# Attention and GELU layer on one core: the first matrix's sums right behind its casts, loads in the weights' buffers, temporaries in unread weights

## The chip, the core and the metric

The kernel runs on one core of a Trainium2 chip. Its engines work side by side, each on its own instruction stream: PE (TensorE, matmuls), DVE (VectorE), ACT (ScalarE), POOL (GpSimd) and SP (SyncE, which here only issues DMAs). They meet at semaphores. PE writes to PSUM, of which the kernel uses eight buffers in turn; the other engines move results from there to SBUF. The metric is the device time of one execution in microseconds.

## The reference

Two layers one behind the other. First a linear attention with decay, in 4 batches, 8 heads, 768 positions, 64 channels, blocks of 64 positions:

```python
for b in range(nb):
    intra = einsum(qb, kb) * Dmask              # scores inside the block, masked with powers of lam
    intra = einsum(intra, vb)
    inter = einsum(qb * lam_pow, kv_state)      # what earlier blocks left
    out[block] = intra + inter
    kv_state = lam_block * kv_state + einsum(kb * rev_pow, vb)
```

Then a dense layer pair on its output x (3072 tokens of 512 features), with a hidden width of 2048:

```python
h = x @ w_in                                    # 512 x 2048
g = 0.5 * h * (1.0 + tanh(c * (h + 0.044715 * h * h * h)))
return g @ w_out                                # 2048 x 512, float32
```

## The kernel before

**Steps.** The attention goes through 24 steps. A step is half of the heads (four) over 256 positions, two chunks of 128. `load_step` brings q, k and v of a step in float32 (256 KB each, 2 KB in each partition), by three DMAs from SP. `cast_q` (DVE, L282) and `cast_k` (ACT, L295) make float16 of q and k, `scale_v` (POOL, L266) of v. q and k are transposed by PE (`stage_t`, L321, for steps up to 7) or by a transposing DMA (L303, from step 8). `scores` (L350) gives S = k q; `causal` (DVE, L360) multiplies by the mask and writes the float16 tile PT. `products` (L385 to L408) or, for two steps at once, `burst` (L436 to L461) multiplies v by PT and adds the state's part. `update` makes the next state t (DVE, L503 and L506) and its float16 form u (POOL, L513). `x_out` (ACT, L487) writes x transposed.

**Groups.** The dense layers go in seven groups of steps. Both matrices are cast to float16 once (`cast_win`, L110 and L108; `cast_wout`, L118 and L120). Group 0 multiplies plainly. From group 1 the second product is done with seven block products in place of eight (`product`, L640), for which sums of blocks of w_out are made (`sum_wout`, L133), and sums of the GELU's output (`sum_g`, L610). In groups 5 and 6 the first product goes the same way (`seven`, L739): it needs four sums of blocks of w_in, each made in two parts on DVE (`sum_win`, L151, eight instructions on 128x1024), sums of blocks of x (`sum_x`, L718), and temporaries that carry partial results between the seven products (`copied`, L751 and L753; `added`, L761). Which blocks it reads is in a table, by (columns half, rows half) or by the number of a sum:

```python
I_SUMS = {1: ((1, 0), ALU.add, (1, 1)), 2: (1, ALU.subtract, (0, 0)),
          3: ((0, 0), ALU.subtract, (1, 0)), 4: ((0, 1), ALU.subtract, 2)}
X_FACTORS = {1: ((0, 0), (0, 0)), 2: ((0, 1), (1, 0)), 3: (4, (1, 1)), 4: ((1, 1), 4),
             5: (1, 1), 6: (2, 2), 7: (3, 3)}
```

**Order.** Nothing is planned automatically: every instruction is pinned to the program order of its engine, and the order is written out by hand at the end of the kernel. The dense layers' pieces lie in a list, `filler`; `fill(n)` emits the next n of them between the parts of the attention, so that PE has work while other engines prepare a step. Dependencies between engines are found by the framework from the regions that the instructions touch.

**Buffers.** A pool hands out tiles by tag; a new tile takes the buffer of an old one of the same tag when all accesses to that one are done. Before, q, k and v have four buffers each (tags q32, k32, v32 of pool `ld`, 24 KB in each partition). The float32 weights arrive in `wst`, four tags of 8 KB: w_in's column quarters in w0 to w3, then w_out's row quarters 0, 2, 1, 3 in w0, w1, w2, w3. Later w0 and w1 hold the sums of the GELU, w2 and w3 the sums of w_in (`ws`). The temporaries of `seven` rotate through q32 and k32. Loads up to step 8 stand at the head of SP's order, behind the weights.

Of the kernel before, what the change touches and what calls it, by code (L numbers as in the profile page):

```python
# [8 lines left out]
FP32 = mybir.dt.float32  # L9
FP16 = mybir.dt.float16  # L10
AF = mybir.ActivationFunctionType
ALU = mybir.AluOpType
# [3 lines left out]
def kernel(  # L16
# [10 lines left out]
    nc = tc.nc  # L27
    pin = tc.keep_in_program_order
    P = 128
    B, H, S, D = q.shape  # L30
    SB = 256
    NSB = S // SB
    HH = H // 2
    DM = H * D
    DFF = moe_w_in.shape[1]
# [6 lines left out]
    const = ctx.enter_context(tc.tile_pool(name="const", bufs=1))  # L42
    w16p = ctx.enter_context(tc.tile_pool(name="w16", bufs=1))
    wst = ctx.enter_context(tc.tile_pool(name="wst", bufs=1))
    ld = ctx.enter_context(tc.tile_pool(name="ld", bufs=4))
    a16p = ctx.enter_context(tc.tile_pool(name="a16", bufs=5))
    qkp = ctx.enter_context(tc.tile_pool(name="qkp", bufs=5))
    ptp = ctx.enter_context(tc.tile_pool(name="ptp", bufs=3))
    ucp = ctx.enter_context(tc.tile_pool(name="ucp", bufs=3))
    ubp = ctx.enter_context(tc.tile_pool(name="ubp", bufs=4))  # L50
    xtp = ctx.enter_context(tc.tile_pool(name="xtp", bufs=3))
    gtp = ctx.enter_context(tc.tile_pool(name="gtp", bufs=2))
    mtp = ctx.enter_context(tc.tile_pool(name="mtp", bufs=1))
# [4 lines left out]
    ld32 = {}  # L58

    def load_step(s, names="qkv"):  # L60
        b, r = divmod(s, 2 * NSB)
        sb, half = divmod(r, 2)
        ts = ld32.setdefault(s, [])
        for nm, src in (("q", q), ("k", k), ("v", v)):
            if nm not in names:
                continue
            t = ld.tile([P, HH, 2, D], FP32, tag=nm + "32", name=f"{nm}32_{s}")
            rows = src[b, half * HH : (half + 1) * HH, sb * SB : (sb + 1) * SB, :]
            queue = nc.scalar if (nm, s) == ("v", 0) else nc.sync
            pin(queue.dma_start(out=t[:].rearrange("p h j d -> p h (j d)"),  # L70
                                in_=rows.rearrange("h (p j) d -> p h (j d)", j=2)))
            ts.append(t)

    w_in16 = w16p.tile([P, NC, DFF], FP16)
    w_out16 = w16p.tile([P, NF, DM], FP16)
# [2 lines left out]
    HF, HE = NF // 2, DM // 2  # L78
# [65 lines left out]
    def sum_win(m, j, eng):  # L144

        if not wi_sum:
            wi_sum.extend(wst.tile([P, 2, 2, DFF // 2], FP16, tag=f"w{2 + i}", name=f"ws{i}")
                          for i in range(2))
        a, op, b = I_SUMS[m]
        cs, fs = slice(0, 2), slice(512 * j, 512 * j + 512)  # L150
        pin(eng.tensor_tensor(w_in_block(m, cs, fs), w_in_block(a, cs, fs),  # L151
                              w_in_block(b, cs, fs), op))
# [96 lines left out]
    def wide(t):  # L249
        return t.rearrange("p j h d -> p h j d")  # L250

    def decay(t, s):
        hs = halves[s % 2]
        return t[:, hs, :].unsqueeze(3).to_broadcast([P, HH, 2, D])
# [8 lines left out]

    def scale_v(s):
        tv = a16p.tile([P, 2, HH, D], FP16, tag="v16", name=f"v16_{s}")
        pin(nc.gpsimd.tensor_tensor(wide(tv[:]), ld32[s][2][:], decay(dv, s), ALU.mult))  # L266
        a16[s] = a16[s] + (tv,)

    def prep_qk(s):
# [5 lines left out]
        cast_k(s)  # L275

    def cast_q(s):
        q32 = ld32[s][0]
        tqk = a16p.tile([P, 2, 2, HH, D], FP16, tag="qk16", name=f"qk16_{s}")
        tq, tk = tqk[:, 0], tqk[:, 1]  # L280
        q_eng = nc.gpsimd if s == 3 else nc.vector
        pin(q_eng.tensor_tensor(wide(tq), q32[:], decay(dq, s), ALU.mult))  # L282
        if s == 0:
            inverse(halves[0])
            odd(halves[1])
            inverse(halves[1])
        a16[s] = (tq, tk)
        whole_qk[s] = tqk

    def cast_k(s):  # L290
        tk, k32 = a16[s][1], ld32[s][1]
        if s == 4:
            pin(nc.vector.tensor_copy(out=wide(tk), in_=k32[:]))
        else:
            pin(nc.scalar.activation(out=wide(tk), in_=k32[:], func=AF.Copy))  # L295

    whole_qk = {}

# [245 lines left out]
    def queue_group(g, lead=0, per_set=0):  # L544
# [177 lines left out]
        def release():  # L722
            while pending:
                pending.pop(0)()

        def seven(m, k):

            st = of_set.setdefault(k, {})
            for name in {1: "X" if k == 0 else "XW", 2: "W", 5: "Y"}.get(m, ""):
                key = name + str(k % 2) if name == "X" else name  # L730
                if key not in hbank:
                    hbank[key] = ps_M.tile([P, 2, SB], FP32, tag="M", name="H" + name)
                st[name] = hbank[key]
            dst = st[{2: "W", 5: "Y", 3: "Y"}.get(m, "X")]
            a, b = X_FACTORS[m]
            for i in range(2):
                f = 2 * k + i
                for c in range(2):
                    pin(nc.tensor.matmul(  # L739
                        dst[:, i, :],  # L740
                        w_in_block(a, slice(c, c + 1), slice(f * P, f * P + P))[:, 0],
                        x_block(b, slice(c, c + 1))[:, 0],
                        start=((m in (1, 5) or (m, k) == (2, 0)) and c == 0 and i == 0),
                        stop=(m in (2, 3, 4) and c == 1),
                        skip_group_check=True))

            def copied(name, tag, eng):
                t = ld.tile([P, HH, 2, D], FP32, tag=tag, name=f"{name}_{g}_{k}")
                t = t[:].rearrange("p h j d -> p (h j d)").rearrange("p (i t) -> p i t", i=2)
                if eng is nc.scalar:  # L750
                    pin(nc.scalar.activation(out=t, in_=dst[:], func=AF.Copy))  # L751
                else:
                    pin(eng.tensor_copy(out=t, in_=dst[:]))  # L753
                st[name] = t

            def gelu(F, T, src):
                pin(nc.scalar.activation(out=gT[:, 2 * k : 2 * k + 2, F, T * SB : T * SB + SB],  # L757
                                         in_=src, func=AF.Gelu_apprx_tanh))

            def added(F, T, name):  # L760
                pin(nc.vector.tensor_tensor(st[name], dst[:], st[name], ALU.add))  # L761
                pending.append(lambda src=st[name]: gelu(F, T, src))

            if m == 1 and k == 0:
                copied("m1", "q32", nc.scalar)
            elif m == 1:
                pin(nc.scalar.activation(out=st["W"][:], in_=dst[:], func=AF.Copy))
            elif m == 2 and k == 0:  # L770
                added(0, 0, "m1")
            elif m == 2:
                pending.append(lambda: gelu(0, 0, dst[:]))
            elif m == 5:
                copied("q", "q32", nc.scalar)
                release()
            elif m == 6:
                copied("u2", "k32", nc.vector)
                release()
            elif m == 3:  # L780
                added(0, 1, "u2")
            elif m == 7:
                added(1, 1, "q")
            elif m == 4:
                pending.insert(0, lambda: gelu(1, 0, dst[:]))
            if k == HF // 2 - 1 and m in (3, 7, 4):
                release()

# [193 lines left out]
    cast_win(2, 0, 256, 128)  # L982
    cast_win(2, 256, 512)
    cast_win(3)
    DVE, ACT, POOL = nc.vector, nc.scalar, nc.gpsimd
    cast_wout(0, (POOL, POOL))
    fill(8)
# [38 lines left out]
    for n, (a, b, c, d) in FILL.items():  # L1026
        stage_t(n)
        fill(a + (n == 10))
        if n == 8:
            cast_q(n + 2)  # L1030
            fill(1)
            cast_k(n + 2)
            transpose_dma(n + 2)
        else:
            prep_qk(n + 2)
        if n < 11:
            load_step(n + 4, "qkv" if n < 10 else "qk")
        if n == 9:
            store_pair(1)
        if n == 11:  # L1040
            scale_v(13)
            load_step(14, "v")
            load_step(16, "qk")
        elif n == 9:
            scale_v(11)
        elif n == 10:
            scale_v(12)
            load_step(15, "qk")
        elif n == 12:
            scale_v(14)  # L1050
        fill(b + (n == 8) - (n == 10))
        R(n, n - 1, keep=n == 8)
        fill(c)
        if n == 8:
            update(n, 0)
            scale_v(n + 2)
            fill(2)
        U(n)
        if n == 12:
            prep_qk(15)  # L1060
            load_step(15, "v")
            load_step(16, "v")
            scale_v(15)
        fill(d)
        if n > 8:
            sum_win((n - 7) // 2, (n - 1) % 2, nc.vector)

    cast_qk(16)
    load_step(17, "qk")
# [21 lines left out]
    fill(1)  # L1091
    U(17)
    fill(1)
    sum_win(3, 0, nc.vector)
    fill(2)
    prep(19)
    sum_win(3, 1, nc.vector)
    fill(2)
    sum_win(4, 0, nc.vector)
    fill(2)  # L1100
    sum_win(4, 1, nc.vector)
    fill(2)
    prep_qk(20)
    fill(1)
# [56 lines left out]
```

## Time and profile before

| | |
|---|---|
| runs of the kernel | 198.87, 198.85, 200.48 us; median 198.87 |
| the profiled execution | 198.79 us, of it 197.0 in the span |
| PE's granted clock | 1.00 |
| busy: PE, DVE, ACT, POOL | 97%, 76%, 61%, 38% of the span |
| HBM read and written | 27.26 MB and 6.29 MB |

The span is the stretch from the first to the last recorded instruction. A view of groups has one row for each line of the kernel, engine and operation; "idle before" is the time that the engine waited just ahead of it, with what ended the wait. A timeline merges like instructions that follow each other: start, duration of all, engine, line, what is written from what, the count, and in brackets the idle time before. The chain of work that ended last is followed back from the last instruction; it names for each stretch of time the work that set the end. Instructions of one engine overlap by some hundredths of a microsecond, so the distance from start to start is a little less than a duration. PEld is PE's loading of the stationary operand. SPq is the issuing of a DMA by SP.

### The profile page before, as it was taken

Reading aid. Unit: us, or ns where it says so; the run is one execution under the profiler, and the core shown is the slowest. Engines: PE = TensorE matmul, PEld = TensorE weight load, DVE = VectorE, ACT = ScalarE, POOL = GpSimd, SP = SyncE. Lnnn points to the kernel's source line nnn. Section 1 sums busy time; section 2 is a strip of 40 time slices with the busy share of each in tenths; the row PEclk is TensorE's granted clock in tenths of the full one; section 3 lists DMA queues with packets and bytes.
Section 4 is the critical chain, followed back from the end, with each engine's and each line's share of the span. In section 5 each row is a group of like instructions: output and inputs, shape, how many; then the busy total and the mean of one; then the engine's idle time right before and its main releaser. Section 6 shows DMA issues by size and latency. Waiting matters only on the chain.

```text
span 197.0 us, 5913 instructions
## 1 busy us (share of the span) xinstructions
PE 191.2 (97%) x2431; PEld 140.1 (71%) x2431; DVE 149.0 (76%) x291; ACT 121.1 (61%) x249; POOL 74.4 (38%) x85
## 2 busy tenths in 40 slices
PE   8979999999999999999999999999999999999993
PEld 2556544446888888654688764578888888888882
DVE  4797722889999889859999927999656987487620
ACT  3663878357874685686845378844867746679221
POOL 6594213457554931169754517165002030002000
PEclk9999999999999999999999999999999999999999
DMA  5999999999999999999996998400211300020205
GB/s 167 292 324 384 387 383 386 300 285 297 259 220 248 257 333 231 213 238 288 226 294 132 274 310 202 92 7 0 53 67 42 107 6 2 0 110 29 77 19 198
DMA packets 62810, 38.13 MB, mean 194 GB/s; under 512 B 18624, under 2 KB 55744, under 8 KB 62784
## 3 DMA queue, kind: packets, MB, share of 16 engines
q1 hardware_dynamic: 62240, 37.50, 74.3%
q8 instruction: 19, 0.31, 0.7%
q10 hardware_dynamic: 544, 0.26, 0.5%
q14 instruction: 7, 0.06, 0.1%
HBM read 27.26 MB, written 6.29 MB: 170 GB/s over the span
## 4 chain that ended last, share of the span: by engine, by line
PE 89%; SPq 4%; DMA 4%; ACT 0%; issue 0%
PE Hps L561 25%; PE MX L640 18%; PE MY L640 9%; PE HX L739 7%; PE O2ps L576 7%; PE MW L640 4%; DMA wi<-in_moe_w_in_dram 4%; SPq L70 4%; PE HY L739 4%; PE S L350 3%; PE Hps L838 3%; PE HW L739 2%; PE OK L408 2%; PE O L461 1%; PE O L436 1%; PE OK L399 1%
## 5 line engine op out<-in xcount | busy, mean ns | idle before, releaser
L561 PE MATMUL Hps<-xT,w_in 128*128 128x512 f16 (+1 forms) x288 | 50.5, 332 | 0.0
L513 POOL TENSOR_TENSOR u<-t,lumask 128x256 f16<-128x256 f32 x40 | 30.9, 788 | 40.7 <-DVE t L506 27.0
L561 PEld LDWEIGHTS <-w_in 128*128 128x128 f16 x288 | 27.9, 98 | 19.1
L565 ACT ACTIVATE gT<-Hps 128x512 f16<-128x512 f32 x56 | 33.5, 598 | 11.6 <-PE Hps L561 11.1
L360 DVE TENSOR_TENSOR PT<-S,mask 128x512 f16<-128x512 f32 x48 | 30.3, 680 | 7.8 <-PE S L350 7.8
L266 POOL TENSOR_TENSOR v<-v,dv 128x512 f16<-128x512 f32 x24 | 28.7, 1197 | 15.2 <-DMA v<-in_v_dram 14.0
L640 PEld LDWEIGHTS <-gs 128*128 128x128 f16 x320 | 31.2, 98 | 3.6
L640 PEld LDWEIGHTS <-gT 128*128 128x128 f16 x240 | 23.3, 98 | 3.2 <-ACT gT L565 0.2
L640 PE MATMUL MX<-w_sum,gs 128*128 128x256 f16 x160 | 21.4, 273 | 0.0
L692 POOL TENSOR_TENSOR o<-u,q 128x512 f32<-128x512 f32 (+1 forms) x5 | 6.3, 1252 | 36.7 <-ACT u L657 36.7
L282 DVE TENSOR_TENSOR qk<-q,dq 128x512 f16<-128x512 f32 x23 | 19.1, 833 | 0.8 <-DMA q<-in_q_dram 0.7
L295 ACT ACTIVATE qk<-k 128x512 f16<-128x512 f32 x23 | 14.4, 625 | 7.4 <-DMA k<-in_k_dram 7.3
L610 DVE TENSOR_TENSOR gs<-gT 128x1024 f16<-128x1024 f16 (+1 forms) x24 | 16.9, 711 | 1.6 <-ACT gT L565 1.6
L576 PE MATMUL O2ps<-w_out,gT 128*128 128x512 f16 x64 | 14.6, 379 | 0.0
L487 ACT ACTIVATE xT<-OK 128x256 f16<-128x256 f32 x26 | 9.9, 452 | 7.0 <-PE OK L408 6.5
L739 PEld LDWEIGHTS <-ws 128*128 128x128 f16 x128 | 12.5, 98 | 1.6 <-issue 0.2
L487 ACT ACTIVATE xT<-O 128x256 f16<-128x256 f32 x22 | 8.0, 461 | 5.8 <-PE O L461 4.9
L657 ACT ACTIVATE u<-MX 128x256 f32<-128x256 f32 x18 | 6.9, 384 | 7.4 <-PE MX L640 7.3
L576 PEld LDWEIGHTS <-gT 128*128 128x128 f16 x64 | 6.1, 98 | 6.6
L350 PEld LDWEIGHTS <-qkT 64*64 64x64 f16 x384 | 6.0, 106 | 6.8 <-issue 3.6
L640 PE MATMUL MY<-w_out,gs 128*128 128x256 f16 x80 | 10.7, 273 | 0.0
L753 DVE COPY u<-HX 128x512 f32<-128x512 f32 x8 | 5.5, 688 | 6.8 <-ACT gT L757 4.3
(98 smaller groups left out, 318.4 us busy)
## 6 DMA issues: line engine op xcount, KB each, us to landing
q<-in_q_dram SPq DMA_DIRECT2D x24, 256.0 KB, 4.9
k<-in_k_dram SPq DMA_DIRECT2D x24, 256.0 KB, 5.0
v<-in_v_dram SPq DMA_DIRECT2D x23, 256.0 KB, 5.2
out_dram<-o SPq DMA_DIRECT2D x23, 256.0 KB, 4.3
wo<-in_moe_w_out_dram SPq DMA_DIRECT2D x4, 1024.0 KB, 9.4
wi<-in_moe_w_in_dram SPq DMA_DIRECT2D x4, 512.0 KB, 7.1
wi<-in_moe_w_in_dram SPq DMA_DIRECT2D x2, 1024.0 KB, 12.5
v<-in_v_dram ACTq DMA_DIRECT2D x1, 256.0 KB, 4.3
```

The lines of the kernel that those rows point to most:

```text
L266: pin(nc.gpsimd.tensor_tensor(wide(tv[:]), ld32[s][2][:], decay(dv, s), ALU.mult))
L282: pin(q_eng.tensor_tensor(wide(tq), q32[:], decay(dq, s), ALU.mult))
L295: pin(nc.scalar.activation(out=wide(tk), in_=k32[:], func=AF.Copy))
L360: pin(nc.vector.tensor_tensor(t[:, hl].rearrange("p b c d -> p b (c d)"), Sps[:].rearrange("p b c d -> p b (c d)"), mask[:].unsqueeze(1).t ...
L487: pin(nc.scalar.activation(out=d, in_=o, func=AF.Copy))
L513: pin(nc.gpsimd.tensor_tensor(u[:], state[half][:].unsqueeze(2).to_broadcast([P, 2, 2, D]), lumask[:, 2 * half : 2 * half + 2, :].unsqueez ...
L561: pin(nc.tensor.matmul(by_block(Hps[:, i, :]), w_in16[:, c, f * P : (f + 1) * P], x(c), start=(c == 0), stop=(c == NC - 1)))
L565: pin(nc.scalar.activation(out=dst, in_=Hps[:], func=AF.Gelu_apprx_tanh))
L576: pin(nc.tensor.matmul(O2[tau][0][:], gT[:, f % HF, f // HF, tau * P : (tau + 1) * P], w_out16[:, f, :], start=(n == 0), stop=(n == NF - 1)))
L610: pin(nc.vector.tensor_tensor(g_rows(m, i), g_rows(a, i), g_rows(b, i), op))
L640: pin(nc.tensor.matmul(dst, lhsT, rhs, start=(opens and i == 0), stop=(closes and i == HF - 1), skip_group_check=True))
L739: pin(nc.tensor.matmul(dst[:, i, :], w_in_block(a, slice(c, c + 1), slice(f * P, f * P + P))[:, 0], x_block(b, slice(c, c + 1))[:, 0], sta ...
```

## The change

**Sums.** The eight instructions of `sum_win` were spread over the order: one each at the ends of steps 9 to 12 and four between the pieces behind `U(17)`. They now stand together behind `cast_win(3)`, ahead of `cast_wout(0)`. Their tiles `ws0` and `ws1` move from the tags w2 and w3 to the buffers in which steps 2 and 3 were loaded.

**Loads.** q, k and v of a step share one tile of 6 KB. Steps 0 to 3 have tags a to d of `ld`, one buffer each. Later steps with s % 4 of 0 or 1 use a and b again; those with 2 or 3 use w2 and w3 of the weights' pool, behind w_out's quarters 1 and 3. c and d grow to 8 KB for the sums. The order of the DMAs stays.

**Temporaries.** `copied` no longer takes a tile. m1 and q lie in the block of w_in16 with rows half 0 and columns half 1, u2 in the block of w_out16 with rows half 0 and columns half 1, which the seven products don't read. `quarters` gives operands of the same four-dimensional form.

**Buffer counts.** `ld` now takes 28 KB of each partition in place of 24. PT goes from three buffers to two (2 KB), t from three to two for each half (1 KB), u from four to three for each half (1 KB).

```diff
-    ld = ctx.enter_context(tc.tile_pool(name="ld", bufs=4))
+    ld = ctx.enter_context(tc.tile_pool(name="ld", bufs=1))
...
-    ptp = ctx.enter_context(tc.tile_pool(name="ptp", bufs=3))
-    ucp = ctx.enter_context(tc.tile_pool(name="ucp", bufs=3))
-    ubp = ctx.enter_context(tc.tile_pool(name="ubp", bufs=4))
+    ptp = ctx.enter_context(tc.tile_pool(name="ptp", bufs=2))
+    ucp = ctx.enter_context(tc.tile_pool(name="ucp", bufs=2))
+    ubp = ctx.enter_context(tc.tile_pool(name="ubp", bufs=3))
...
-        ts = ld32.setdefault(s, [])
-        for nm, src in (("q", q), ("k", k), ("v", v)):
+        if s not in ld32:
+            pool, tag = ((ld, "abcd"[s % 4]) if s < 4 or s % 4 < 2 else (wst, f"w{s % 4}"))
+            ld32[s] = [pool.tile([P, 3, HH, 2, D], FP32, tag=tag, name=f"qkv32_{s}")]
+        for i, (nm, src) in enumerate((("q", q), ("k", k), ("v", v))):
             if nm not in names:
                 continue
-            t = ld.tile([P, HH, 2, D], FP32, tag=nm + "32", name=f"{nm}32_{s}")
+            t = ld32[s][0][:, i]
...
-            wi_sum.extend(wst.tile([P, 2, 2, DFF // 2], FP16, tag=f"w{2 + i}", name=f"ws{i}")
+            wi_sum.extend(ld.tile([P, 2, 2, DFF // 2], FP16, tag="cd"[i], name=f"ws{i}")
                           for i in range(2))
...
+        def quarters(t):
+            return t.rearrange("p i (a t) -> p i a t", a=2)
+
+        def held(name, i):
+            if name == "q":
+                t = w_in16[:, i, DFF // 2 : DFF].bitcast(FP32)
+                return t.rearrange("p (i a t) -> p i a t", i=2, a=2)
+            t = w_out16[:, 4 * i : 4 * i + 4, HE : 2 * HE].bitcast(FP32)
+            return t.rearrange("p (i a) t -> p i a t", a=2)
...
-            def copied(name, tag, eng):
-                t = ld.tile([P, HH, 2, D], FP32, tag=tag, name=f"{name}_{g}_{k}")
-                t = t[:].rearrange("p h j d -> p (h j d)").rearrange("p (i t) -> p i t", i=2)
+            def copied(name, eng):
+                st[name] = t = held(name, 1 if name == "m1" else k % 2)
...
     cast_win(3)
+    for m in I_SUMS:
+        for j in range(2):
+            sum_win(m, j, nc.vector)
...
-        if n > 8:
-            sum_win((n - 7) // 2, (n - 1) % 2, nc.vector)
...
-    sum_win(3, 0, nc.vector)
     fill(2)
     prep(19)
-    sum_win(3, 1, nc.vector)
     fill(2)
-    sum_win(4, 0, nc.vector)
     fill(2)
-    sum_win(4, 1, nc.vector)
     fill(2)
```

More of the change, by code (lines that the diff above doesn't have):

```diff
@@ L62, in load_step @@
         sb, half = divmod(r, 2)
-        ts = ld32.setdefault(s, [])
-        for nm, src in (("q", q), ("k", k), ("v", v)):
+        if s not in ld32:
+            pool, tag = ((ld, "abcd"[s % 4]) if s < 4 or s % 4 < 2 else (wst, f"w{s % 4}"))
+            ld32[s] = [pool.tile([P, 3, HH, 2, D], FP32, tag=tag, name=f"qkv32_{s}")]
+        for i, (nm, src) in enumerate((("q", q), ("k", k), ("v", v))):
             if nm not in names:
                 continue
-            t = ld.tile([P, HH, 2, D], FP32, tag=nm + "32", name=f"{nm}32_{s}")
+            t = ld32[s][0][:, i]
             rows = src[b, half * HH : (half + 1) * HH, sb * SB : (sb + 1) * SB, :]
             queue = nc.scalar if (nm, s) == ("v", 0) else nc.sync
-            pin(queue.dma_start(out=t[:].rearrange("p h j d -> p h (j d)"),
+            pin(queue.dma_start(out=t.rearrange("p h j d -> p h (j d)"),
                                 in_=rows.rearrange("h (p j) d -> p h (j d)", j=2)))
-            ts.append(t)
     w_in16 = w16p.tile([P, NC, DFF], FP16)
@@ L265, in scale_v @@
         tv = a16p.tile([P, 2, HH, D], FP16, tag="v16", name=f"v16_{s}")
-        pin(nc.gpsimd.tensor_tensor(wide(tv[:]), ld32[s][2][:], decay(dv, s), ALU.mult))
+        pin(nc.gpsimd.tensor_tensor(wide(tv[:]), ld32[s][0][:, 2], decay(dv, s), ALU.mult))
         a16[s] = a16[s] + (tv,)
@@ L277, in cast_q @@
     def cast_q(s):
-        q32 = ld32[s][0]
+        q32 = ld32[s][0][:, 0]
         tqk = a16p.tile([P, 2, 2, HH, D], FP16, tag="qk16", name=f"qk16_{s}")
@@ L281, in cast_q @@
         q_eng = nc.gpsimd if s == 3 else nc.vector
-        pin(q_eng.tensor_tensor(wide(tq), q32[:], decay(dq, s), ALU.mult))
+        pin(q_eng.tensor_tensor(wide(tq), q32, decay(dq, s), ALU.mult))
         if s == 0:
@@ L290, in cast_k @@
     def cast_k(s):
-        tk, k32 = a16[s][1], ld32[s][1]
+        tk, k32 = a16[s][1], ld32[s][0][:, 1]
         if s == 4:
-            pin(nc.vector.tensor_copy(out=wide(tk), in_=k32[:]))
+            pin(nc.vector.tensor_copy(out=wide(tk), in_=k32))
         else:
-            pin(nc.scalar.activation(out=wide(tk), in_=k32[:], func=AF.Copy))
+            pin(nc.scalar.activation(out=wide(tk), in_=k32, func=AF.Copy))
     whole_qk = {}
@@ L745, in seven @@
                         skip_group_check=True))
-            def copied(name, tag, eng):
-                t = ld.tile([P, HH, 2, D], FP32, tag=tag, name=f"{name}_{g}_{k}")
-                t = t[:].rearrange("p h j d -> p (h j d)").rearrange("p (i t) -> p i t", i=2)
+            def copied(name, eng):
+                st[name] = t = held(name, 1 if name == "m1" else k % 2)
                 if eng is nc.scalar:
-                    pin(nc.scalar.activation(out=t, in_=dst[:], func=AF.Copy))
+                    pin(nc.scalar.activation(out=t, in_=quarters(dst[:]), func=AF.Copy))
                 else:
-                    pin(eng.tensor_copy(out=t, in_=dst[:]))
-                st[name] = t
+                    pin(eng.tensor_copy(out=t, in_=quarters(dst[:])))
             def gelu(F, T, src):
-                pin(nc.scalar.activation(out=gT[:, 2 * k : 2 * k + 2, F, T * SB : T * SB + SB],
-                                         in_=src, func=AF.Gelu_apprx_tanh))
+                to = gT[:, 2 * k : 2 * k + 2, F, T * SB : T * SB + SB]
+                pin(nc.scalar.activation(out=quarters(to), in_=src, func=AF.Gelu_apprx_tanh))
             def added(F, T, name):
-                pin(nc.vector.tensor_tensor(st[name], dst[:], st[name], ALU.add))
+                pin(nc.vector.tensor_tensor(st[name], quarters(dst[:]), st[name], ALU.add))
                 pending.append(lambda src=st[name]: gelu(F, T, src))
             if m == 1 and k == 0:
-                copied("m1", "q32", nc.scalar)
+                copied("m1", nc.scalar)
             elif m == 1:
@@ L772, in seven @@
             elif m == 2:
-                pending.append(lambda: gelu(0, 0, dst[:]))
+                pending.append(lambda: gelu(0, 0, quarters(dst[:])))
             elif m == 5:
-                copied("q", "q32", nc.scalar)
+                copied("q", nc.scalar)
                 release()
             elif m == 6:
-                copied("u2", "k32", nc.vector)
+                copied("u2", nc.vector)
                 release()
@@ L784, in seven @@
             elif m == 4:
-                pending.insert(0, lambda: gelu(1, 0, dst[:]))
+                pending.insert(0, lambda: gelu(1, 0, quarters(dst[:])))
             if k == HF // 2 - 1 and m in (3, 7, 4):
```

## The prediction

> **What bounds the kernel now.** I read the page's busy times first, then the chain of work that ended last in order of time, then the waits, then the timelines of single engines. The profiled execution took 198.79 us, of which the span is 197.0, so 1.8 lies around the span. The median of the three runs is 198.87. About 1% of that, 1.99 us, is what a measurement of this kernel can tell from no change.
>
> From the page:
>
> ```profile
> PE 191.2 (97%) x2431; PEld 140.1 (71%) x2431; DVE 149.0 (76%) x291; ACT 121.1 (61%) x249; POOL 74.4 (38%) x85
> ```
>
> A busy PE may still hide stalls, so I went to the chain (start, duration, what):
>
> ```profile
> 9.86 7.88 DMA wi<-in_moe_w_in_dram
> 17.77 0.42 ACT w_in L108
> 18.24 1.13 PE Hps L838 x8
> ...
> 24.41 6.91 PE Hps L561 x32
> 31.32 7.77 PE O2ps L576 x36
> 39.09 0.45 PE Tps L321 x8
> ...
> 137.21 0.44 PE MX L640 x4
> 137.65 0.59 PE HX L739 x4
> 138.24 0.44 PE MX L640 x4
> ...
> 193.76 0.38 ACT o L657
> ```
>
> The reader is to see three stages. Up to 17.8 us a weight load sets the end. From 18.24 to 193.74 it is PE in every piece, and piece touches piece. [...] 32 products of 512 columns in 6.91 us are 216 ns each, 8 of 256 columns in 0.87 us are 109 ns. Four of 256 columns take 0.44 us almost everywhere, and 0.59 at 137.65: 0.15 us of stall. The change leaves PE's instructions as they are, so in 175 us there are a few tenths to gain. What remains is to ask where it makes PE wait.
>
> [...] the trace's plain cases of 128x1024 take 0.68 us each, 0.60 from start to start (two in 1.28). [...] POOL's casts of this size take 1.0 us with DVE idle (two in 2.02) and 1.45 beside such sums, and one of the sums to be moved (107.62) took 1.52 beside a POOL scaling of 1.49.
>
> **Part 1: the eight sums (L151) move to behind the casts.** They cost 3.9 + 1.4 + 1.3 = 6.6 us where they are (66 to 111 us), and leave there. PE does not wait for DVE in that stretch, so their going is worth nothing in time. Their new place on DVE is behind the last cast of the first matrix. DVE, then POOL there (start, duration, idle before and its releaser):
>
> ```profile
> 25.86 1.29 DVE L110 CAST w_in<-wi 128x1024 f16<-128x1024 f32 x2 [1.35 <-DMA wi<-in_moe_w_in_dram]
> 30.64 0.69 DVE L133 TENSOR_TENSOR w_sum<-w_out 128x1024 f16<-128x1024 f16 x1 [3.50 <-POOL w_out L120]
> 33.87 0.69 DVE L133 TENSOR_TENSOR w_sum<-w_out,w_sum 128x1024 f16<-128x1024 f16 x1 [2.53 <-ACT w_out L118]
> ...
> 37.73 0.92 DVE L282 TENSOR_TENSOR qk<-q,dq 128x512 f16<-128x512 f32 x1 [0.53 <-DMA q<-in_q_dram]
> ```
> ```profile
> 28.59 2.02 POOL L120 CAST w_out<-wo 128x1024 f16<-128x1024 f32 x2 [6.49 <-DMA wo<-in_moe_w_out_dram]
> 34.01 1.45 POOL L120 CAST w_out<-wo 128x1024 f16<-128x1024 f32 x1 [3.40 <-DMA wo<-in_moe_w_out_dram]
> ```
>
> DVE sits idle 3.50 + 2.53 + 0.53 = 6.56 us between 27.1 and 37.7. Eight sums at 0.60 are 4.8, so 27.1 to 31.9; the two POOL casts from 28.59 beside them cost DVE 0.23 (two sums of the second matrix took 1.52 in place of 1.29 beside one) to 0.84 each (the 1.52 at 107.62), so the end is 32.4 to 33.6. The first sum of the second matrix then ends by 34.2 and the next, which waited for ACT until 33.87, is 0 to 0.35 late, and the wait for the q load of step 4 (0.53) takes that up. Behind these on DVE are the step's q and k casts, for which PE's transposes at 39.09 wait; they end at 38.65 and 39.07, so this stage has a margin of little more than 0.2 us beyond that. I take 0 for it.
>
> The other party is POOL: its two casts feed PE's products at 31.32, and the second pair of rows is read by the third product, at 31.32 + 2 x 0.216 = 31.75. The casts end at 28.59 + 2.02 = 30.61 now; with 0.45 more each (1.45 against 1.0) at 31.5. That still fits, by 0.25 us. Bounds: 0 to 0.3; I take 0.
>
> **Part 2: where the loads land.** Steps 2 and 3 of each four now use the weights' buffers. The load of step 6 must wait for the casts of w_out's second quarter (ACT ends at 35.04, POOL at 35.46); SP issues it at 37.63 in any case. That of step 7 must wait for POOL's last cast (38.10); SP issues it at 40.30 (start, time of issue):
>
> ```profile
> 37.63 0.83 SPq L70 DMA_DIRECT2D q<-in_q_dram  x1
> ...
> 40.30 0.78 SPq L70 DMA_DIRECT2D q<-in_q_dram  x1
> ```
>
> SP is held there by earlier loads, since all 16 DMA engines are busy, so 2.2 us of margin stay in both. A step's three loads now share one tile, so that a load waits for all three readers of the old one, the v scaling on POOL included. I went through them: step 8 is issued at 42.76, the scaling of 4 ends at 40.6; 16 at 79.81 against 69.2 (of 12); 18 at 91.36 against 84.7; 23 at 119.37 against 108.6. None is late. Nothing behind them on SP, the transposing DMAs and the stores, moves later: 0.
>
> **Part 3: temporaries of the last two groups in unread blocks of the weights.** Same instructions, same element counts (0.69 us on DVE, 0.6 on ACT). The unread blocks interleave with blocks that PE reads. If the dependencies were kept for whole tiles, PE would wait after each copy. The chain excludes it: L561 starts at 24.41 on columns of w_in16, while the casts of other columns of the same tile, written earlier in program order, run until 27.15. 0.
>
> **Part 4: one buffer less for PT, t and u.** For t and u I followed each chain of one half: a buffer comes back when POOL, or a product, has read the value two (t) or three (u) before. All these reads lie a step or more earlier. PT is different. In burst() the masks of steps 20 and 21 come behind the products that read PT of 18 and 19, and with two buffers PT of 20 is PT of 18's. The burst at 125 us, and where it ends up on DVE:
>
> ```profile
> 125.07 0.64 PE L350 MATMUL S<-qkT 64*64 64x128 f16 x32
> 125.53 2.48 DVE L360 TENSOR_TENSOR PT<-S,mask 128x512 f16<-128x512 f32 x4
> 125.54 0.62 PE L436 MATMUL O<-PT,v 64*64 64x128 f16 x32
> ...
> 136.92 0.67 DVE L753 COPY u<-HX 128x512 f32<-128x512 f32 x1
> ```
>
> The first mask starts at 125.53, when the products that read PT have only begun. The 32 take 0.62 and each 0.22, so their starts spread over 0.40; the 16th, the last for step 18, ends near 125.54 + 0.20 + 0.22 = 125.96. So the mask is 0.45 late (bounds 0.3, if the wait ends on the first products' tick, to 0.6, if it ends with the last of the 32 at 126.16). Behind it DVE works without a gap until 137.59: t, the four sums of x, the sums of the GELU, and the copy of HX at 136.92, for which PE waits at 137.65 (the 0.15 us seen above). So the delay reaches PE whole: +0.45. After that copy DVE idles 1.78 us and is level again. In the bursts at 94 and 117 us the same happens (0.40 and 0.47), but DVE's next products there are due 3 us later, or 1.05 us of idle follow; at 88 and 155 PT has been read in time. If POOL's v scalings (2.94 us for two, beside DVE there) fall otherwise against DVE's sums, part of it may go or double: 0.1 to 0.9.
>
> **The sum.** 0 + 0 + 0 + 0.45: the execution of 198.79 becomes 199.24, and on the median of 198.87 it is 199.3.
>
> **Rivals.**
> - *Nothing moves* (the PT delay is swallowed by another phase of DVE against POOL, and the freed DVE removes the 0.15): 198.7. For it: 0.45 us is small against 12 us of DVE work that contention stretches. Against it: that work has no gap.
> - *The start runs over its cover*: POOL's casts come 0.3 late for the products at 31.75 and the DVE stream 0.4 late for step 4, beside the 0.45 of PT: 200.0. For it: margins of 0.25 us; against: each takes the worst contention of the trace.
> - *DVE is late as a whole at step 4* (the slower side). Should the sums average 1.5 us, as the worst did, they end at 27.1 + 12 = 39.1; the five sums of the second matrix (3.1) follow, and q's cast starts at 42.2 in place of 37.73. Less 0.2 of margin PE loses 4.2 us: 203. It decides from 0.85 us a sum, where the 6.56 us of idle are used up, and passes 1% at some 1.1. Against it: only two POOL casts lie beside the eight sums.
> - *PE gains*: the scaling and casting of steps 11 to 21 come up to 3 us earlier. For a gain of 1% there would have to be a stall in PE's chain there, and there is none: not over 0.3, so 198.5.
>
> **How the numbers follow.** Chances: forecast 0.47 (its own range 198.9 to 199.8), nothing moves 0.20, the start over its cover 0.15, DVE late 0.14 (from 200.9 up), a gain 0.04 (0.03 of it over 1%, by what I have not seen). The range 198.4 to 201.2 takes the first three and the near end of the fourth. Faster 0.03, within 1% 0.83, slower 0.14.
>
> **What would show it.** Right: L151 at 27 to 33 us; the first idle times of DVE before L133 gone; PE unbroken at 31.75 and 39.1; the PT groups at 94, 117 and 125 starting 0.4 to 0.5 later, with a wait for the products O; the HX piece near 137.65 at about 1.0 us; SP's loads of steps 6 and 7 where they were. Wrong: a PE wait for w_out's casts or for q of step 4 of a microsecond or more, a wait of loads for v's scaling, PE waiting for ACT or DVE in each set of the last two groups, or a span shorter by over 0.3 us.

## The result, and the profile after

The changed kernel takes 199.77 us in the median (199.32 to 200.26, 20 runs), the kernel before beside it 198.88. The ratio is 1.0036, with a 95% interval of 1.0018 to 1.0053: slower by 0.36%, or 0.7 us (0.4 to 1.1). By the two medians it is 0.9 us: ratio and quotient of medians differ by up to 0.2 us in these runs, so terms of a tenth are read from the spans below. The loss is within the 1% that the prediction took as the least that can be told from no change, yet 20 runs do tell it. The median is 0.5 us above the predicted 199.3 and just inside the forecast's own range, 198.9 to 199.8.

Every run comes with its span, so the loss can be split at once. In the medians of these runs the span is 197.7 us after and 197.1 before (58 runs of it in the last experiments; a 59th took 394.04 us, twice as long, and is left out), and what lies around the span is 2.09 us after and 1.79 before. So there are two terms: 0.6 us inside the span and 0.3 outside. The prediction had only the first.

The page after: PE's instructions are the same, and DVE is no busier than before.

```profile
PE 191.7 (97%) x2431; PEld 140.2 (71%) x2431; DVE 148.0 (75%) x291; ACT 121.2 (61%) x249; POOL 72.6 (37%) x85
```

The chain of work that ended last, in order of time. Its columns are start, duration, what:

```profile
18.38 1.14 PE Hps L850 x8
...
31.46 7.77 PE O2ps L579 x36
39.23 0.62 PE Tps L324 x8
...
116.57 0.57 PE S L353 x32
...
121.02 0.61 ACT gT L568
121.65 1.27 DVE gs L613
...
126.15 0.55 DVE PT L363
...
137.64 0.61 DVE w_out L766
138.29 0.60 PE HX L753 x4
138.89 0.44 PE MX L643 x4
```

PE starts its dense work 0.14 us later than before (18.38 against 18.24: a weight load took 8.11 in place of 7.88), and at 116.57 it is still 0.16 behind. The change need not be the reason for this: in run 8 below, which has the old loads and sums, the same weight load takes 8.12. At the HX piece the distance is 0.64 (138.29 against 137.65), and it stays so to the end (ACT's last copy starts at 194.41 against 193.76). The further loss of 0.5 us is set at this one piece. And the chain says by whom: from 121 to 138 us it no longer runs over PE but over DVE, from a sum of the GELU (gs) through the masks (PT) to the copy of u2, here named w_out because the temporary lies there. (By `held` in the change, m1 lies in w_out16 as well; of the temporaries only q is in w_in16.)

PE's own waits, us in total, times, longest, have a row that was not there before:

```profile
PE HX L753 <- DVE w_out L766: 0.4, 1, 0.4
```

The start of the kernel, DVE and then POOL:

```profile
27.20 1.29 DVE L154 TENSOR_TENSOR ws<-w_in 128x1024 f16<-128x1024 f16 x2
28.40 2.12 DVE L154 TENSOR_TENSOR ws<-ws,w_in 128x1024 f16<-128x1024 f16 x2
30.45 2.12 DVE L154 TENSOR_TENSOR ws<-w_in 128x1024 f16<-128x1024 f16 x2
32.49 1.28 DVE L154 TENSOR_TENSOR ws<-w_in,ws 128x1024 f16<-128x1024 f16 x2
33.70 0.68 DVE L136 TENSOR_TENSOR w_sum<-w_out 128x1024 f16<-128x1024 f16 x1
...
37.87 1.20 DVE L285 TENSOR_TENSOR qk<-qkv,dq 128x512 f16<-128x512 f32 x1 [0.24 <-DMA qkv<-in_q_dram]
```
```profile
28.71 2.71 POOL L123 CAST w_out<-wo 128x1024 f16<-128x1024 f32 x2 [6.46 <-DMA wo<-in_moe_w_out_dram]
```

The eight sums fill the hole in which DVE had waited. Two of the four pairs take 2.12 in place of 1.29: each lost 0.83 to one of POOL's two casts. In the kernel before, a cast (34.01 to 35.46) had cost one sum of the second matrix as much, 1.52 in place of 0.68:

```profile
34.48 1.52 DVE L133 TENSOR_TENSOR w_sum<-w_out 128x1024 f16<-128x1024 f16 x1
```

The eight sums are done at 33.8, DVE still waits 0.24 for the q load, and the casts end at 31.42, ahead of the product at 31.9 that reads them.

Where the lateness begins, DVE around the bursts and then POOL's v scaling (brackets: idle before, and its releaser). First the kernel before:

```profile
116.80 2.48 DVE L360 TENSOR_TENSOR PT<-S,mask 128x512 f16<-128x512 f32 x4 [3.58 <-PE S L350]
...
121.48 0.80 DVE L610 TENSOR_TENSOR gs<-gT 128x1024 f16<-128x1024 f16 x1 [1.05 <-ACT gT L565]
```
```profile
120.70 1.04 POOL L266 TENSOR_TENSOR v<-v,dv 128x512 f16<-128x512 f32 x1
```

And the changed kernel:

```profile
117.42 2.48 DVE L363 TENSOR_TENSOR PT<-S,mask 128x512 f16<-128x512 f32 x4 [6.58 <-PE O L439]
...
121.65 1.26 DVE L613 TENSOR_TENSOR gs<-gT 128x1024 f16<-128x1024 f16 x1 [0.59 <-ACT gT L568]
...
125.48 0.68 DVE L285 TENSOR_TENSOR qk<-qkv,dq 128x512 f16<-128x512 f32 x1
126.15 2.48 DVE L363 TENSOR_TENSOR PT<-S,mask 128x512 f16<-128x512 f32 x4
```
```profile
121.32 1.04 POOL L269 TENSOR_TENSOR v<-qkv,dv 128x512 f16<-128x512 f32 x1
```

The masks at 117.42 now wait for O, the products that read PT, and no longer for S; they start 0.62 later than before (0.16 of it is common). The prediction had seen this and put it aside, since 1.05 us of idle follow. But this idle ends with an event of ACT, and POOL, which works behind DVE's t, came later too: its v scaling lies at 121.32 to 122.36 (before: 120.70 to 121.74), over the sum at 121.65, which takes 1.26 in place of 0.80. So half a microsecond (0.46) gets past the idle time as contention, and at 126.15 DVE comes late to the masks by itself, with no wait for O left to see. Two causes then lie on top of each other; runs 3 and 4 take them apart.

### The profile page after: what moved, and what is told of

It reads as the page before. It is cut to its first block, busy times and chain, and to the rows that moved or that the text cites. A ratio compares the mean times of both kernels' runs of the same rounds, so it can differ in the third digit from the quotient of the medians.

```text
span 197.7 us, 5908 instructions
## 1 busy us (share of the span) xinstructions
PE 191.7 (97%) x2431; PEld 140.2 (71%) x2431; DVE 148.0 (75%) x291; ACT 121.2 (61%) x249; POOL 72.6 (37%) x85
## 4 chain that ended last, share of the span: by engine, by line
PE 80%; DVE 7%; SPq 4%; DMA 4%; issue 1%; ACT 1%; DVEq 0%
PE Hps L564 21%; PE MX L643 16%; PE MY L643 8%; PE O2ps L579 7%; PE HX L753 7%; DMA wi<-in_moe_w_in_dram 4%; SPq L74 4%; PE MW L643 4%; DVE gs L613 3%; PE HY L753 3%; PE S L353 3%; PE Hps L850 3%; PE OK L411 2%; PE HW L753 2%; PE OK L402 1%
## 5 line engine op out<-in xcount | busy, mean ns | idle before, releaser
L516 POOL TENSOR_TENSOR u<-t,lumask 128x256 f16<-128x256 f32 x40 | 30.3, 770 | 43.5 <-DVE t L509 31.4
L269 POOL TENSOR_TENSOR v<-qkv,dv 128x512 f16<-128x512 f32 x24 | 27.5, 1148 | 15.2 <-DMA qkv<-in_v_dram 13.5
L695 POOL TENSOR_TENSOR o<-u,q 128x512 f32<-128x512 f32 (+1 forms) x5 | 5.7, 1139 | 36.8 <-ACT u L660 36.8
L298 ACT ACTIVATE qk<-qkv 128x512 f16<-128x512 f32 x23 | 14.4, 625 | 6.9 <-DMA qkv<-in_k_dram 6.8
L613 DVE TENSOR_TENSOR gs<-gT 128x1024 f16<-128x1024 f16 (+1 forms) x24 | 17.4, 730 | 1.6 <-ACT gT L568 1.6
L285 DVE TENSOR_TENSOR qk<-qkv,dq 128x512 f16<-128x512 f32 x23 | 17.4, 755 | 0.6 <-DMA qkv<-in_q_dram 0.5
L613 DVE TENSOR_TENSOR gs<-gT,gs 128x1024 f16<-128x1024 f16 (+1 forms) x12 | 10.6, 883 | 0.7 <-DVE gs L613 0.5
L686 DVE TENSOR_TENSOR o<-MY,u 128x512 f32<-128x512 f32 (+1 forms) x6 | 3.6, 600 | 9.9 <-PE MY L643 9.2
```

Of the source, the lines that this page charges most:

```text
L269: pin(nc.gpsimd.tensor_tensor(wide(tv[:]), ld32[s][0][:, 2], decay(dv, s), ALU.mult))
L285: pin(q_eng.tensor_tensor(wide(tq), q32, decay(dq, s), ALU.mult))
L298: pin(nc.scalar.activation(out=wide(tk), in_=k32, func=AF.Copy))
L516: pin(nc.gpsimd.tensor_tensor(u[:], state[half][:].unsqueeze(2).to_broadcast([P, 2, 2, D]), lumask[:, 2 * half : 2 * half + 2, :].unsqueez ...
L613: pin(nc.vector.tensor_tensor(g_rows(m, i), g_rows(a, i), g_rows(b, i), op))
```

## The experiments

All are compared with the kernel before on the same chip, by ratio and interval; the median of the kernel before was 198.84 in each set. "Outside" is the time less the span, in the median. Each kernel has 14 to 22 runs, except the second of runs 3 and 4 (5 runs) and that of run 6 (6 runs).

**1. Three PT buffers in the changed kernel.**

```diff
-    ptp = ctx.enter_context(tc.tile_pool(name="ptp", bufs=2))
+    ptp = ctx.enter_context(tc.tile_pool(name="ptp", bufs=3))
...
-                    st[name] = mtp.tile([P, NP, HE], FP32, tag=name, name=name)
+                    st[name] = mtp.tile([P, NP, HE], FP32, tag="m1" if name == "u3" else name, name=name)
```

> The changed kernel with three buffers for PT again (room for the third: u3 and m1, two temporaries of the seven products that are never alive together, share a buffer). Theory, the PT wait sets the loss: the PT groups at 117 and 126 us start 0.5 to 0.6 earlier, the HX piece near 138 us is back at about 0.6 us, and the time falls by 0.5 to 0.6 against the changed kernel, to within 0.2 of the kernel before. Rival, the loss is in the loads or in the sums at the start: at most 0.1 comes back.

Measured: 199.16, ratio 1.0012 (1.0003 to 1.0022); span 197.15, outside 2.00. The masks, and the piece that had waited:

```profile
116.84 2.48 DVE L363 TENSOR_TENSOR PT<-S,mask 128x512 f16<-128x512 f32 x4 [6.20 <-PE S L353]
121.53 0.81 DVE L613 TENSOR_TENSOR gs<-gT 128x1024 f16<-128x1024 f16 x1 [1.04 <-ACT gT L568]
125.57 2.48 DVE L363 TENSOR_TENSOR PT<-S,mask 128x512 f16<-128x512 f32 x4
```
```profile
137.71 0.60 PE HX L753 x4
```

The wait is for S again, the sum takes 0.81, and the HX piece is back where it was. The span is that of the kernel before to 0.05 us. What stays, 0.2 us by the ratio and 0.3 by the medians, lies outside the span. The smaller counts of t and u are still in this kernel, so they cost nothing in the span.

**2. Two PT buffers in the kernel before.**

```diff
-    ptp = ctx.enter_context(tc.tile_pool(name="ptp", bufs=3))
+    ptp = ctx.enter_context(tc.tile_pool(name="ptp", bufs=2))
```

> The kernel before with two buffers for PT in place of three, nothing else. Theory PT: slower by 0.5 to 0.7 us, with the wait of PT for the products O at 117 us and a longer HX piece near 138 us. Rival (loads, sums or temporaries): within 0.1 of the kernel before.

Measured: 199.37, ratio 1.0024 (1.0016 to 1.0032); span 197.6, so 0.5 more, and outside 1.78, as before. In its profile the masks wait for O at 117, and the HX piece comes at 138.33:

```profile
117.49 2.48 DVE L360 TENSOR_TENSOR PT<-S,mask 128x512 f16<-128x512 f32 x4 [2.82 <-PE O L436]
121.72 1.27 DVE L610 TENSOR_TENSOR gs<-gT 128x1024 f16<-128x1024 f16 x1 [0.58 <-ACT gT L565]
126.21 2.49 DVE L360 TENSOR_TENSOR PT<-S,mask 128x512 f16<-128x512 f32 x4
```

So the count of PT buffers alone makes 0.5 us of span, in both directions.

**3. and 4. Which burst?** With the room that run 1 found, one step can have a PT buffer of its own. In the first kernel that is step 20, so that only the wait at 126 us goes; in the second, steps 18 and 20 share it, so that only the one at 117 goes.

```diff
-        t = ptp.tile([P, 2, 2, 2, P], FP16, tag="PT", name=f"PT_{n}")
+        own = dict(tag="PT20", bufs=1) if n == 20 else dict(tag="PT")
+        t = ptp.tile([P, 2, 2, 2, P], FP16, name=f"PT_{n}", **own)
...
```

The second has `own = dict(tag="PT18", bufs=1) if n in (18, 20) else dict(tag="PT")`. The cut part lets u3 and m1 share a buffer, as in run 1.

> The changed kernel with a buffer of its own for PT of step 20 alone, so that only the wait of the burst near 126 us goes and those at 94 and 117 us stay. If the loss comes in at 126 us, as predicted: as with three buffers, 0.5 to 0.6 back. If the lateness of the burst at 117 us passes through (its u on POOL then collides with DVE's sums at 121.6, whose first took 1.26 us in place of 0.80): PT of step 20 still starts near 126.1 and nothing, at most 0.1, comes back.

> The changed kernel with a PT buffer that steps 18 and 20 share and two for the others: the wait of the burst at 117 us goes (nothing holds PT of 18), that of the burst at 126 stays (PT of 20 waits for the products that read 18's). With the two runs on PT this completes the square. If each wait is enough by itself: the PT group at 117 starts at 116.9, the sum at 121.6 takes 0.8 again, q's cast ends at 125.7, yet PT of 20 waits for O until about 126.1, and at most 0.15 us comes back. If the burst at 117 us is the only one that counts: 0.4 to 0.6 comes back.

Measured: 199.50, ratio 1.0030 (1.0020 to 1.0040), span 197.5; and 199.74, ratio 1.0046 (1.0034 to 1.0058), span 197.7. The first gives back 0.2 us of span, somewhat more than the 0.1 that was expected at most, the second nothing. The first kernel's timeline of DVE, then the second's:

```profile
121.71 1.26 DVE L614 TENSOR_TENSOR gs<-gT 128x1024 f16<-128x1024 f16 x1 [0.59 <-ACT gT L569]
126.13 2.47 DVE L364 TENSOR_TENSOR PT<-S,mask 128x512 f16<-128x512 f32 x4
```
```profile
116.99 2.48 DVE L364 TENSOR_TENSOR PT<-S,mask 128x512 f16<-128x512 f32 x4 [6.03 <-PE S L353]
121.68 0.80 DVE L614 TENSOR_TENSOR gs<-gT 128x1024 f16<-128x1024 f16 x1 [1.05 <-ACT gT L569]
126.18 2.48 DVE L364 TENSOR_TENSOR PT<-S,mask 128x512 f16<-128x512 f32 x4 [0.45 <-PE O L440]
```

Without a wait at 126 DVE arrives late there all the same, by the 1.26 of the sum. Without the lateness from 117 it arrives in time, and waits 0.45 for O: the figure of the prediction. Each is enough alone. (The expectation of the first run blamed u for the collision; it is the v scaling just ahead of it.)

**5. The far end: u2's first copy in group 5 on ACT.**

```diff
-                copied("u2", nc.vector)
+                copied("u2", nc.scalar if (g, k) == (5, 0) else nc.vector)
```

> The changed kernel with the first copy of u2 in group 5 (the one that PE waits for near 138 us) on ACT in place of DVE; ACT is idle for about 0.8 us just there. If that one wait is where the lateness of DVE reaches PE: the HX piece starts near 137.7 as PE is ready and the time falls by 0.5 to 0.65 us against the changed kernel, while the PT groups stay as late as they are. If DVE's lateness reaches PE elsewhere too: less than 0.3.

Measured: 199.07, ratio 1.0002 (0.9986 to 1.0018); span 197.1, 0.6 less than with the change alone, outside 2.0. The masks stay late (117.51 and 126.27 in the profile), yet the piece takes 0.44, as nearly all of its form do:

```profile
127.05 2.72 PE Hps L564 x12
...
138.06 0.44 PE HX L753 x4
```

So nearly all of DVE's lateness reaches PE at this one wait. A small part does so earlier: the Hps piece at 127 us, behind the burst, takes 2.72 here and 2.59 in the kernel before, 0.13 more. In the changed kernel the longer wait for the copy of u2 covers that; with both ends undone (run 10) the piece takes 2.59 again, and the span is 0.1 us shorter than here.

**6. The sums back at their old places.** The rest is as changed; only the calls of `sum_win` stand where they stood.

> The changed kernel with the eight sums of the first matrix back at their old places in the order (their buffers as changed). If the sums behind the casts are covered: same as the changed kernel within 0.15 us, L133's waits of 3.5 and 2.5 us back. If they cost by the crowded start (the transposes of step 4 took 0.62 in place of 0.45): 0.2 faster. If they help DVE later on: slower by 0.1 to 0.5.

Measured: 199.50, ratio 1.0042 (1.0028 to 1.0057); span 197.6, outside 1.96. DVE waits 3.5 and 2.6 us for the casts of w_out again, and PE's chain gains nothing to speak of (0.1 us of span at most): the transposes of step 4 take 0.45 in place of 0.62, but PE is at S of step 6 at 47.52 against 47.53. The transposes of step 5, which wait in any case (0.66 us here, 0.55 with the sums at the start), swallow the difference.

**7. One tile for each step's loads, and the temporaries, in the kernel before.**

```diff
...
+        if s not in ld32:
+            ld32[s] = [ld.tile([P, 3, HH, 2, D], FP32, tag="qkv", name=f"qkv32_{s}")]
...
-            t = ld.tile([P, HH, 2, D], FP32, tag=nm + "32", name=f"{nm}32_{s}")
+            t = ld32[s][0][:, i]
...
```

The cut parts are the readers of the tile and the temporaries, as in the change.

> The kernel before with one tile for the q, k and v of a step (four of them in turn, none in the weights' buffers) and the temporaries in the unread blocks of the weights; the sums and the counts of PT, t and u as before. As predicted for these two parts: within 0.1 us of the kernel before, and PE's chain unbroken. Rival: about 0.2 us slower, which is what stayed when PT had three buffers, seen in the time outside the span (1.8 us before, 2.0 after) and not in PE's chain.

Measured: 199.05, ratio 1.0015 (1.0005 to 1.0024); span 197.05, outside 2.01. The chain is unbroken, the span is the old one, and the 0.2 us are outside.

**8. The temporaries alone in the kernel before.**

> The kernel before with the temporaries in the unread blocks of the weights, nothing else. As predicted: no difference, within 0.1 us. If the 0.15% by which the run with one tile for each step and these temporaries was slower lies here: 0.2 slower; if it lies in the loads: none here.

Measured: 198.86, ratio 0.9993 (0.9980 to 1.0005); span 197.1, outside 1.78. So the temporaries are free, and what run 7 lost came with its one tile for each step.

**9. Three PT buffers and the sums spread.** At that time I read the time outside the span from one profiled execution of each kernel and took it for a matter of the sums' place.

> The changed kernel with three PT buffers and the eight sums at their old places; what stays of the change is the loads, the temporaries and the counts of t and u. In the profiles so far the time outside the span is 2.0 to 2.1 us wherever the sums stand behind the casts (six kernels) and 1.75 to 1.79 elsewhere (four). If the rest of 0.24 us that three PT buffers left belongs to the sums' place: within 0.1 us of the kernel before, and 1.8 us outside the span. If it belongs to the loads or the temporaries: still 0.2 slower.

Measured: 199.19, ratio 1.0015 (1.0002 to 1.0028); span 197.1, outside 2.10. That theory falls: the sums are spread, and the time outside is as long as ever. A single execution misleads here (the profiled ones of run 6 and run 7 show 1.8, others of the same kernels up to 2.04 and 2.11). Taken over all runs, the split is by the loads:

| kernel | loads | median outside the span, us |
|---|---|---|
| before | three tiles | 1.77 to 1.79 |
| before, two PT buffers | three tiles | 1.78 |
| before, temporaries | three tiles | 1.78 |
| before, u2 on ACT | three tiles | 1.78 |
| before, loads and temporaries | one tile | 2.01 |
| changed | one tile | 2.09 |
| changed, with any of the other edits (eight kernels) | one tile | 1.96 to 2.12 |

**10. Both ends undone, and the attempt at a better kernel.** Three kernels carry u2's copy on ACT: the changed one with three PT buffers, the same with the sums spread, and the kernel before.

> The changed kernel with three PT buffers and the first copy of u2 of group 5 on ACT, so that both ends of the found chain are undone. If the two are one chain, the gains don't add: about the time of each alone less the 0.15 us of stall that the kernel before had, 198.8 to 199.0 and at best level with the kernel before. If they are independent: another 0.5 us, 198.5.

> The same with the first copy of u2 in group 5 on ACT: the best that these edits can give. PE's stall near 138 us (0.15 in the kernel before) goes too: 198.7, 0.15 better than the kernel before. If the edits hide no stall but that one, not more.

> The kernel before with the first copy of u2 in group 5 on ACT, nothing else: the HX piece near 137.6 at 0.44 in place of 0.59, the span shorter by 0.15 us, 198.7. Rival: ACT is late in its own queue there and the stall stays or grows.

Measured: 199.06, ratio 1.0011 (1.0004 to 1.0018), span 197.0; 198.89, ratio 1.0000 (0.9989 to 1.0011), span 196.9; 198.89, ratio 1.0000 (0.9990 to 1.0010), span 197.1. The gains of the two ends don't add: it is one chain. In all three profiles the HX piece, 0.59 in the kernel before, takes 0.44, as here in the kernel before with the copy on ACT:

```profile
137.68 0.44 PE HX L739 x4
```

In the changed kernels with three PT buffers the end of this stall shows in the span: about 0.15 us with the sums at the start (197.0 against run 1's 197.15) and 0.2 with the sums spread (196.9 against run 9's 197.1). In the kernel before it doesn't. There the profile has ACT's last copy 0.13 earlier (193.63 against 193.76), but from the end of this copy to the end of the span it is 3.1 us in place of 2.9; why is open. Both kernels for which 198.7 was expected took 198.89. No version beats the kernel before.

## Why the prediction was right, and where it was not

- *In 175 us of PE's chain there are a few tenths to gain* held. That its products could go no faster than 216 ns at 512 columns and 109 at 256 was the author's estimate: the trace shows that they keep this pace (32 of 512 take 6.91 us at 24.41 and again at 118.23, eight of 256 take 0.87), not that it is the least. The freed DVE (6.6 us of sums gone from the stretch at 66 to 111 us) brought nothing, and the one stall that could be removed was worth no measurable time in the kernel before, at most 0.2 us of span elsewhere (run 10).
- *Part 1, the sums: 0* held (run 6). The sums' end at 32.4 to 33.6 came at 33.8, the casts' end at 31.5 at 31.42. DVE lost 0.83 for each POOL cast, the upper end of the bounds. The lower end, 0.23, rested on a wrong reading: the 1.52 us at 34.48 in the kernel before are one sum (x1), not two. The margin at step 4 was overrun by 0.17 us; that it would be made up for two pieces later was not in the sum. So the 0 for this stage was right by a slack that the prediction hadn't counted.
- *Part 2, the loads: 0* held inside the span: SP issued q of steps 6 and 7 at 37.83 and 40.44, 2.6 and 1.9 us behind the casts that it must wait for (2.2 both by the prediction). That SP is held up because the DMA engines are busy was the author's estimate; the profile before shows them busy for 9 tenths or more from 30 to 45 us, and single issues of loads that take up to 2.62 us there. The prediction failed outside the span. The time around the span was taken as a constant 1.8, and with one tile for each step it is 2.0 to 2.1. This is the missing term of the sum, 0.2 to 0.3 us, which had been put at nothing without a reason.
- *Part 3, the temporaries: 0* held (run 8).
- *Part 4, one PT buffer less: 0.45* measured 0.5 (run 2: the span grew by 0.5), at the place and over the path that were named: PT late, 12 us of DVE without a gap, the copy of u2, PE's HX piece. Two of the signs named did not come in that form: at 126 us no wait for O was left to see, and the HX piece came late instead of taking 1.0 us. The step "or 1.05 us of idle follow" was wrong for the burst at 117 us. Its delay passes the idle time by meeting POOL's v scaling, and is a second sufficient cause (runs 3 and 4). The size didn't suffer, since two causes of the same lateness don't add. That was in part luck: the missed cause passes on just the 0.46 us by which the burst at 117 came late, about the 0.45 of the wait at 126. In the kernel before, one sum lost 0.84 us to POOL (1.52 in place of 0.68, at 34.48); with that much, by the author's estimate, the missed cause would have set the loss. The smaller counts of t and u cost nothing in the span, as predicted (runs 1 and 9).
- *The rivals.* "Nothing moves" rested on contention swallowing the delay, and contention carried it further. The start did run over its cover, by 0.17 us, without effect. DVE was not late as a whole at step 4: a moved sum took 0.82 in the mean (6.6 us for eight), just under the 0.85 from which that case decides.

The sum with the terms as measured: 0.5 for PT and 0.2 to 0.3 outside the span give 0.7 to 0.8, against 0.7 by the ratio and 0.9 by the medians. The 0.1 us of span that is left by the medians is not assigned to a part of the change.

## What to carry to other kernels

PE's chain was closed here but for a few tenths, and none of the 13 other kernels, all with the same PE instructions, was measurably faster (ratios 0.9993 to 1.0046). With such a chain look for the new waits: a buffer count that goes down by one makes a writer wait for the readers of two rounds ago in place of three, and where program order puts the writer just behind these readers, that wait comes (0.4 to 0.5 us here). Idle time on an engine need not take up a delay: here 1.05 us of it stood behind masks that were 0.46 late by the change, and 0.46 came through, since POOL, which DVE feeds, was shifted onto the next sum. And subtract the span from the time for all runs of a kernel, not for one: the 0.2 to 0.3 us there are in no engine's timeline.

## What the runs showed of the hardware

A DVE sum of two SBUF inputs takes 0.68 us in its plain cases (128x1024 in float16; 35.93 in the kernel before). Four sums took 0.83 to 0.84 more beside a POOL cast or scaling of 1.0 us: two in the changed kernel (2.12 for each pair at 28.40 and 30.45 in place of 1.29), two in the kernel before (1.52 at 34.48 and at 107.62). One at 34.48 in the changed kernel took 0.66 more (1.34), beside a cast of 1.14. The POOL instructions took longer too: 2.71 for the two casts at 28.71 in place of 2.02, 0.35 each, and 1.49 for the scaling at 107.11 in place of 1.04. In the collision at 121 us the scaling, which had started first, kept its 1.04, and the sum took 0.46 more than in the kernel before. This is what the text calls contention; in what the two engines meet, the traces don't show. The 0.83 us is most of the 1.0 us that the POOL instruction takes alone.

With one load tile for each step in place of three, the time outside the span was longer by 0.2 to 0.3 us, with the same DMAs in the same order and an unchanged span (run 7 against run 8, and the table of run 9). No instruction of the program lies there, but DMA packets are recorded: behind the span's end, the traces before and after have two packets of 8 KB each, of the queue that the profile calls "q14 instruction". In the execution before, the last of them starts 0.59 us behind the end, and the time outside is 1.78; in the one after it starts 1.88 behind, and the time outside is 2.13. So in these two the extra time goes with something behind the last instruction. Of the 14 profiled executions six have 1.7 to 1.8 us outside, the other eight 1.9 to 2.1. The six are the four kernels with three tiles, and runs 6 and 7, which have one: a kernel with one tile can show either. The longer time was frequent with one tile (medians of 1.96 to 2.12); with three, the time outside was 1.73 to 1.87 in every run of the experiments. Why one tile brings it about is open; that the program is laid out differently in memory is a rival that was not tested.
